# Rounding the fill's operands on GpSimd instead of VectorE, and turning -max and 1/sum a step later

## The chip, the cores and the metric

The kernel runs on one core of one Trainium2 chip. The core has TensorE (PE, with its weight loads PEld), VectorE (DVE), ScalarE (ACT), GpSimd (POOL) and SyncE (SP), which here issues every transfer. Each engine works through its own queue in order and waits for the others by semaphores. The metric is the device time of one execution in microseconds.

## The reference

Two independent layers share one launch, and their outputs are laid side by side. A is attention with 32 query heads of width 32 and a single key and value head, over 2048 rows of width 1024, followed by an output projection. B is a Fourier mixing layer, written as products with cosine and sine matrices.

```
q = (x @ wq).reshape(B, S, H, Dh).transpose(0, 2, 1, 3)      # H = 32, Dh = 32
k = x @ wk;  v = x @ wv
scores = einsum("bhqd,bkd->bhqk", q, k) * Dh ** -0.5
o = einsum("bhqk,bkd->bhqd", softmax(scores), v)
A = o.transpose(0, 2, 1, 3).reshape(B, S, H * Dh) @ wo

a = einsum("bsd,ed->bse", x, dft_hid_re)
b = einsum("bsd,ed->bse", x, dft_hid_im)
B = einsum("ts,bse->bte", dft_seq_re, a) - einsum("ts,bse->bte", dft_seq_im, b)
out = concatenate([A, B], axis=-1)
```

All inputs and outputs are float32.

## The kernel before, in words

Matrix products are made in a rounded float32 form (F32R in the code). To keep the precision, each operand x is split into a high part, x rounded, and a low part, x minus the high part. A product of two operands is then three products on TensorE: high by high, low by high, high by low.

**The fill.** The projections, both stages of the Fourier layer and the output projection are written as a list of groups. A group is one output tile of 128 x 512 and takes 12 or 24 products. The list runs: q, k and v projections; stage 1 of the Fourier layer (the seven products of STAGE1); stage 2 (the seven of PRODUCTS, each in two halves of eight groups); the output projection. The position in this list, counted in products, is `pos["fill"]`.

**The lines that prepare operands.** Two objects of class Line, RL for right operands (tiles rh, rl) and ML for left operands (mh, ml), carry each item through four steps: load (a transfer into r or m), comb (GpSimd adds or subtracts a second or third source, where the item has several), hi (the high part, by `hi_r` or `hi_m`, which call `cast`), and lo (the low part, a subtraction on GpSimd). Each step is issued when the fill has come within a lead of the item's due position: (40, 40, 14, 8) products for RL, (52, 36, 27, 21) for ML. A left operand is due when it is used, and serves 12 products. A right operand serves all eight groups of its half set, and its due position is spread over the set before. Up to the position START (the first groups) `cast` runs on ScalarE and the low part on VectorE; from there `cast` runs on VectorE and the low part on GpSimd. There are 14 buffers for each of rh and rl, 4 for each of mh and ml, 3 and 2 for the first and second source of r and of m.

**The groups' ends.** When a group's last product is placed, its `post` runs. In the second half of a product of stage 2 VectorE adds the PSUM tile to h, and GpSimd adds h into the one or two running sums y that the product touches, where these already exist. Of the two-source left operands, PRODUCTS[0], [1], [3], [4], [5] have them; two running sums are added in PRODUCTS[3] and [6], one in [1], [2], [4] and [5], none in [0]. Stores are issued nine products after their place (BEHIND).

**Attention around it.** The attention runs in 32 units (four blocks of rows by eight groups of heads) of 32 steps. One step of the main loop makes a scores product (tile pss) for a later unit, of which VectorE takes the negated maximum (tile nm) and ScalarE the row sums by an exponential; and a product of the transposed scores (tile pst) for the current unit, of which ScalarE makes the exponential into p. Every eighth step `pv` multiplies 32 pieces of p with v. Fill products are put between by `level`, equally many in every eight steps, none in the step of a pv. There is a bank of PSUM for a group in work and one for what comes between (`bank`).

**The turning.** The transposed scores need -max of each row along the free dimension, and the output needs 1/sum. `lse_1`, `lse_1b` and `lse_2` work these out on VectorE and ScalarE in tile m2 (m in the profile); `lse_3` turns m2 on TensorE with the identity matrix and copies it to mt on VectorE; `lse_4` sends mt with three transfers from SyncE: high and low part of -max into two rows of qst, and 1/sum to the tensor r_d. A unit's transposed scores start at its step 0, in the main loop's count; `lse_3` stands in step 25 of the unit before, one step after a pv, and `lse_4` in step 27. `inverse` fetches 1/sum at step 16 of the unit itself. `aside` completes a group that is just begun or nearly done before anything else uses a bank.

The class Ordered hands every operation to the scheduler in program order, so that the order of each queue is the order of the calls. It records them all, so the profile gives line 66 for nearly everything, and operations are told apart by their tiles.

Of the kernel before, what the change touches and what calls it, by code (L numbers as in the profile page):

```python
# [87 lines left out]
def tile_kernel(ctx: ExitStack, tc, xT, wq, wkv, wo, xbT, wT, cT, out):  # L88
# [3 lines left out]
    dve = Ordered(tc, nc.vector)  # L92
    gp = Ordered(tc, nc.gpsimd)
# [80 lines left out]
    def cast(to, of):  # L174
        if pos["fill"] < START:
            act.activation(to, of, AF.Copy)
        else:
            dve.tensor_copy(to, of)

    def load_r(it):  # L180
        if it.pre or it.t:
# [37 lines left out]
    def hi_r(it):  # L219
        it.hi = rp.tile([P, W], F32R, name="rh")  # L220
        it.lo = rp.tile([P, W], F32R, name="rl")
        if it.pre:
            fetch(it)
        else:
            cast(it.hi, it.t[0])

    def hi_m(it):
        it.hi = mp.tile([P, 4, P], F32R, name="mh")
        it.lo = mp.tile([P, 4, P], F32R, name="ml")
        if it.pre:  # L230
            fetch(it)
            return
        _, n, w = it.t[0].shape
        it.hi, it.lo = it.hi[:, :n, :w], it.lo[:, :n, :w]
        cast(it.hi, it.t[0])
# [355 lines left out]
    def open_unit(u):  # L591
        b, g = units[u]
        assert ("q", b, g) in ready
        q = qsp.tile([P, 4, W], F32R, name="qst")
        gp.memset(q[96:P].bitcast(F32), 0.0)
        for r, src in enumerate((qh_d, ql_d, qh_d)):
            move(sp, q[r * DH:(r + 1) * DH], src[b][g].rearrange("(h d) c -> d h c", d=DH))
        qst[u] = q
        nm[u] = sm.tile([P, 2, NC], F32, name="nm")
        ls[u] = sm.tile([P, 2, NC], F32, name="ls")  # L600

    def scores(s):
        u, r = divmod(s, SU)
        i, j = divmod(r, 2)
        h, t = divmod(i, 4)
        ps = ps_s.tile([P, 2 * W], F32, name="pss")
        for a in range(2):
            k0 = (2 * j + a) * W
            te.matmul(ps[:, a * W:(a + 1) * W], qst[u][:, h, t * P:(t + 1) * P], kst[:, k0:k0 + W], start=True, stop=True)
        dve.tensor_reduce(nm[u][:, j, i:i + 1], ps, axis=AX.X, op=ALU.max, negate=True)  # L610
        pend[s] = ps

    def row_sums(s):
        if s not in pend:
            return
        ps = pend.pop(s)
        u, r = divmod(s, SU)
        i, j = divmod(r, 2)
        act.activation(ps, ps, AF.Exp, bias=nm[u][:, j, i:i + 1], accum_out=ls[u][:, j, i:i + 1])

    def lse_1(u):
        m = sm.tile([P, NC], F32, name="mm")
        d = sm.tile([P, 2, NC], F32, name="md")
        dve.tensor_tensor(m, nm[u][:, 0], nm[u][:, 1], op=ALU.min)
        for j in range(2):
            dve.tensor_sub(d[:, j], m, nm[u][:, j])
        lse[u] = m, d

    def lse_1b(u):
        act.activation(lse[u][1], lse[u][1], AF.Exp)  # L630

    def lse_2(u):
        m, d = lse[u]
        l = sm.tile([P, NC], F32, name="l")
        m2 = sm.tile([P, 3, NC], F32, name="m2")
        dve.tensor_mul(d, d, ls[u])
        dve.tensor_add(l, d[:, 0], d[:, 1])
        dve.tensor_copy(m2[:, 0].bitcast(F32R), m)
        dve.tensor_sub(m2[:, 1], m, m2[:, 0])
        dve.reciprocal(m2[:, 2], l)  # L640
        lse[u] = m2

    def lse_3(u):
        m2 = lse.pop(u)
        aside()
        pm = bank("psb")
        te.transpose(pm[:3 * NC, :P], m2.rearrange("p a b -> p (a b)"), ident)
        mt = sm.tile([3 * NC, P], F32, name="mt")
        dve.tensor_copy(mt, pm[:3 * NC, :P])
        cur["at"] += 1  # L650
        lse[u] = mt

    def lse_4(u):
        mt = lse.pop(u)
        for a in range(2):
            move(sp, qst[u][96 + a:97 + a].rearrange("o h (t c) -> o (h t) c", c=P), mt[a * NC:(a + 1) * NC])
        sp.dma_start(r_d[u], mt[2 * NC:])
# [45 lines left out]
    def score_step(s):  # L703

        if s < total:
            u, r = divmod(s, SU)
            if r == SU - 6 and u + 1 < len(units):
                open_unit(u + 1)
            scores(s)
        row_sums(s - 1)  # L710
        u, e = divmod(s - SU, SU)
        if 0 <= u < len(units):
            if e == 1:
                lse_1(u)
            elif e == 2:
                lse_1b(u)
            elif e == 3:
                lse_2(u)
            elif e == 5:
                lse_3(u)  # L720
            elif e == 7:
                lse_4(u)


# [11 lines left out]
    for s in range(SU + LEAD):  # L736
        score_step(s)
        take(7)
# [14 lines left out]
    for n in range(total):  # L753
        u, r = divmod(n, SU)
        if n == total - 12:
            w1 = wo_set(1)
            add([o_group(NQ - 1, t, e, ws) for e, ws in ((0, w0), (1, w1)) for t in range(4)])
        score_step(n + SU + LEAD)
        if ends:
            ends.pop(0)()  # L760
        expo(n)
        if r == 16:
            inverse(u)
        if r % 8 == 0 and n:
            pv(*divmod(n // 8 - 1, 4))
        level(n)
# [72 lines left out]
```

## Time and profile before

| | |
|---|---|
| median of 3 runs | 2849.58 us (2846.28 to 2852.26) |
| the profiled execution | 2849.53 us, of which the span is 2847.8 us |
| granted TensorE clock, mean | 0.997 |
| TensorE busy | 2794.1 us, 98% |
| ScalarE busy | 2185.7 us, 77% |
| VectorE busy | 1948.0 us, 68% |
| GpSimd busy | 1212.5 us, 43% |
| the 291 roundings of m on VectorE | 167.1 us, 574 ns each |
| the 214 roundings of r on VectorE | 123.1 us, 575 ns each |
| the 32 transpositions of -max and 1/sum on TensorE | 9.1 us, 286 ns each |

How to read it. A group of instructions is named by engine, operation and "out<-in" with buffer numbers left out, so `mh<-m` is the rounding of a left operand. After the bar stand the busy time, the mean of one in ns, and the idle time of the engine just before these instructions with what ended it. In the list of waits a line gives the waiting engine and tile, the releaser, the total in us, the number of times and the longest. A line of the timeline gives start, duration, engine, instruction, and in brackets the idle time before it. PEld is TensorE's loading of weights, which runs beside its products. The ends of matmuls are modelled, so a busy share of 98% doesn't mean that TensorE never stood still; the steps' pace tells that better.

### The profile page before, as it was taken

To read this page: it belongs to the slowest core of one execution; us is meant where nothing else is said; L and a number is where in the kernel's file an instruction comes from. 1 tells how busy PE (TensorE), PEld (TensorE's weight loads), DVE (VectorE), ACT (ScalarE), POOL (GpSimd) and SP (SyncE) were. 2 spreads that over 40 slices of the span, in tenths; PEclk is the share of its full clock that TensorE was granted. 3 is DMA by queue.
4 is the path that set the end of the run, shared out by engine and by line. 5 is a ranking of instruction groups with operands and counts; after the bars stand their busy time and mean duration, and the time that the engine had idled before them with its cause. 6 is when DMAs were issued, how large, how long until landed. Compare 5 with 4: busy or idle time off the path is not lost.

```text
span 2847.8 us, 39945 instructions
## 1 busy us (share of the span) xinstructions
PE 2794.1 (98%) x13904; PEld 1929.8 (68%) x13904; DVE 1948.0 (68%) x2430; ACT 2185.7 (77%) x3151; POOL 1212.5 (43%) x928
## 2 busy tenths in 40 slices
PE   7999999999999999999999999999999999999999
PEld 5776676767666767676767666666666666667656
DVE  6876677777777777776777677677777676766511
ACT  4578788878787888888888888778788788888740
POOL 1211123454324346555664455766666753520000
PEclk9999999999999999999999999999999999999999
DMA  8865425765576455554552454654555533554445
GB/s 295 294 198 172 149 101 167 237 213 197 193 233 212 163 178 160 154 169 123 170 175 93 134 156 133 200 172 138 176 167 155 174 113 100 160 155 138 126 141 170
DMA packets 315722, 480.83 MB, mean 169 GB/s; under 512 B 33408, under 2 KB 98432, under 8 KB 315520
## 3 DMA queue, kind: packets, MB, share of 16 engines
q1 hardware_dynamic: 315520, 478.28, 52.8%
q8 instruction: 109, 1.79, 0.3%
q14 instruction: 93, 0.76, 0.1%
HBM read 364.12 MB, written 112.98 MB: 168 GB/s over the span
## 4 chain that ended last, share of the span: by engine, by line
PE 83%; DVE 7%; ACT 3%; DMA 3%; issue 2%; POOL 1%; SPq 1%; POOLq 0%; ACTq 0%; DVEq 0%
PE psb L66 53%; PE pss L66 15%; PE pst L66 15%; DVE nm L66 2%; ACT pss L66 1%; ACT p L66 1%; DMA ql<-ql 1%; DVE mh L66 1%; DVE rh L66 1%; DVE ov L66 1%; SPq L66 1%; POOL m L66 0%; DMA r<-s 0%; POOL ml L66 0%; DVE md L66 0%
## 5 line engine op out<-in xcount | busy, mean ns | idle before, releaser
L66 DVE TENSOR_REDUCE nm<-pss 128x1 f32<-128x1024 f32 x1024 | 1248.5, 1221 | 379.4 <-PE pss L66 376.6
L66 ACT ACTIVATE p<-pst 128x1024 f32<-128x1024 f32 x1024 | 1051.9, 1027 | 429.4 <-PE pst L66 426.5
L66 ACT ACTIVATE pss<-pss,nm 128x1024 f32<-128x1024 f32 x1024 | 1113.9, 1088 | 149.1 <-DVE nm L66 142.2
L66 PE MATMUL psb<-rh,mh 128*128 128x512 f32 (+1 forms) x1852 | 731.6, 395 | 12.0 <-ACT rh L66 8.2
L66 PE MATMUL psb<-rh,ml 128*128 128x512 f32 (+1 forms) x1852 | 731.9, 395 | 0.7 <-POOL ml L66 0.7
L66 PE MATMUL psb<-rl,mh 128*128 128x512 f32 (+1 forms) x1852 | 729.9, 394 | 0.3 <-DVE rl L66 0.3
L66 PE MATMUL pss<-kst,qst 128*128 128x512 f32 x2048 | 658.6, 403 | 17.2 <-ACT pss L66 16.6
L66 PE MATMUL pst<-qst,kst 128*128 128x512 f32 x2048 | 659.7, 403 | 10.2 <-ACT p L66 9.2
L66 POOL TENSOR_TENSOR rl<-r,rh 128x512 fp32r<-128x512 f32 x214 | 281.9, 1318 | 736.3 <-DVE rh L66 537.8
L66 POOL TENSOR_TENSOR ml<-m,mh 128x512 fp32r<-128x512 f32 x292 | 383.8, 1315 | 484.4 <-DVE mh L66 247.0
L66 PEld LDWEIGHTS pss<-kst,qst 128*128 128x128 f32 x2048 | 373.0, 188 | 208.2 <-issue 93.9
L66 PE MATMUL psb<-p,v 128*32 128x512 f32 x4096 | 466.5, 596 | 0.6 <-DVE h L66 0.5
L66 PEld LDWEIGHTS pst<-qst,kst 128*128 128x128 f32 x2048 | 372.7, 189 | 136.2 <-ACT p L66 54.5
L66 PEld LDWEIGHTS psb<-rh,mh 128*128 128x128 f32 (+1 forms) x1852 | 347.6, 188 | 97.5 <-ACT rh L66 8.7
L66 PEld LDWEIGHTS psb<-rh,ml 128*128 128x128 f32 (+1 forms) x1852 | 347.6, 188 | 84.1 <-POOL ml L66 1.1
L66 PEld LDWEIGHTS psb<-rl,mh 128*128 128x128 f32 (+1 forms) x1852 | 347.3, 188 | 84.5 <-DVE rl L66 1.6
L66 PEld LDWEIGHTS psb<-p,v 128*32 128x32 f32 x4096 | 120.2, 110 | 277.3 <-issue 258.0
L66 POOL TENSOR_TENSOR m<-m,m 128x512 f32<-128x512 f32 x192 | 252.6, 1316 | 13.2 <-DMA m<-in_cT_dram 7.8
L66 DVE TENSOR_TENSOR ov<-ov,psb 128x512 f32<-128x512 f32 x96 | 66.0, 688 | 265.9 <-PE psb L66 265.7
L66 POOL TENSOR_TENSOR r<-r,r 128x512 f32<-128x512 f32 x112 | 149.0, 1331 | 199.1 <-DMA r<-in_wT_dram 101.7
L66 ACT ACTIVATION_READ_ACCUMULATOR pss<-pss,nm 128x1 f32 x1024 | 208.6, 204 | 0.0
L66 DVE CAST mh<-m 128x512 fp32r<-128x512 f32 x291 | 167.1, 574 | 17.5 <-POOL m L66 10.6
(68 smaller groups left out, 848.6 us busy)
## 6 DMA issues: line engine op xcount, KB each, us to landing
m<-in_cT_dram SPq DMA_DIRECT2D x384, 256.0 KB, 3.7
r<-s SPq DMA_DIRECT2D x192, 256.0 KB, 4.3
y<-y SPq DMA_DIRECT2D x96, 256.0 KB, 4.4
r<-in_wT_dram SPq DMA_DIRECT2D x80, 256.0 KB, 3.8
m<-in_xbT_dram SPq DMA_DIRECT2D x80, 256.0 KB, 4.2
y<-u SPq DMA_DIRECT2D x80, 256.0 KB, 2.9
qst<-qh SPq DMA_DIRECT2D x64, 256.0 KB, 5.5
s<-y SPq DMA_DIRECT2D x64, 256.0 KB, 3.5
```

What stands on the lines that cost most here:

```text
L66: return lambda *a, **k: self.tc.keep_in_program_order(f(*a, **k))
```

## The change

Two things are changed. `cast`, which makes the high parts, runs on GpSimd instead of VectorE from the position START on; its place in the program, the leads and the buffers stay. GpSimd thus makes the high part and, some products later, the low part. And the calls of `lse_3` and `lse_4` come one step later, at e == 6 and 8 in place of 5 and 7, that is in steps 26 and 28.

```diff
     def cast(to, of):
         if pos["fill"] < START:
             act.activation(to, of, AF.Copy)
         else:
-            dve.tensor_copy(to, of)
+            gp.tensor_copy(to, of)
...
             elif e == 3:
                 lse_2(u)
-            elif e == 5:
+            elif e == 6:
                 lse_3(u)
-            elif e == 7:
+            elif e == 8:
                 lse_4(u)
```

All other queues keep their contents; the order on TensorE and SyncE shifts slightly around the moved calls.

## The prediction

> **What bounds the kernel now.** First the page: TensorE is busy nearly everywhere, GpSimd only here and there (its row of slices has 4 to 6 tenths in the second half and 0 at the end).
>
> ```profile
> span 2847.8 us, 39945 instructions
> PE 2794.1 (98%) x13904; PEld 1929.8 (68%) x13904; DVE 1948.0 (68%) x2430; ACT 2185.7 (77%) x3151; POOL 1212.5 (43%) x928
> PE   7999999999999999999999999999999999999999
> POOL 1211123454324346555664455766666753520000
> ```
>
> Then the pace. Every unit of attention (32 steps) makes 32 exponentials of the transposed scores, so stretches bounded by those exponentials compare like with like. The windows below give length, ScalarE's busy time with its count, clock, DMA share.
>
> ```profile
> 900.50:1549.40 648.90, 262.95 (x256) 1.00 0.50 157
> 1549.50:2478.70 929.20, 361.51 (x352) 0.99 0.49 150
> 1714.30:1800.50 86.20, 32.77 (x32) 1.00 0.43 134
> 1800.60:1892.20 91.60, 32.88 (x32) 0.96 0.64 203
> 2227.10:2314.20 87.10, 32.82 (x32) 0.98 0.51 158
> ```
>
> Eight units in the middle take 648.9 us, 81.1 each. The eleven after them take 929.2, where 11 x 81.1 = 892 was due: 37 us are lost there, 10.5 in one unit (1800 to 1892). The 81.1 is paced by TensorE and ScalarE together; what the change can win is above all these 37 us.
>
> Third, the waits of 1780 to 1900 us and the timeline inside it:
>
> ```profile
> POOL y L66 <- DVE h L66: 23.1, 7, 7.2
> ACT pss L66 <- DVE nm L66: 16.6, 6, 3.9
> DVE mh L66 <- POOL m L66: 8.4, 4, 2.7
> POOL r L66 <- DMA r<-s: 7.9, 3, 3.4
> PE pss L66 <- ACT pss L66: 7.0, 3, 3.0
> ```
>
> ```profile
> 1833.17 0.67 DVE L66 TENSOR_TENSOR h<-h,psb 128x512 f32<-128x512 f32 x1
> 1833.92 2.54 POOL L66 TENSOR_TENSOR y<-y,h 128x512 f32<-128x512 f32 x2 [2.09 <-DVE h L66]
> 1836.42 1.29 POOL L66 TENSOR_TENSOR m<-m,m 128x512 f32<-128x512 f32 x1
> 1837.67 1.29 POOL L66 TENSOR_TENSOR ml<-m,mh 128x512 fp32r<-128x512 f32 x1
> 1837.75 1.50 DVE L66 CAST mh<-m 128x512 fp32r<-128x512 f32 x1 [2.68 <-POOL m L66]
> 1839.17 1.21 DVE L66 TENSOR_REDUCE nm<-pss 128x1 f32<-128x1024 f32 x1
> 1840.30 0.41 DVE L66 CAST rh<-r 128x512 fp32r<-128x512 f32 x1
> 1840.47 1.09 ACT L66 ACTIVATE pss<-pss,nm 128x1024 f32<-128x1024 f32 x1 [3.00 <-DVE nm L66]
> 1842.65 0.79 PE L66 MATMUL pst<-qst,kst 128*128 128x512 f32 x2 [0.18 <-ACT p L66]
> ```
>
> This is a ring of two queues. GpSimd waits for VectorE's h at a group's end, adds two y, then the next m; VectorE meanwhile has come to the rounding of that m, stands still for 2.68 us, takes 1.50 us instead of 0.41 for it (GpSimd's other work runs beside), and only then reduces the scores that ScalarE waits 3.00 us for. TensorE waits behind ScalarE. VectorE's total of 68% shows none of it.
>
> **The change, part by part.** The by-shape view has the durations, and two rows to bound a GpSimd copy:
>
> ```profile
> L66 DVE CAST mh<-m 128x512 fp32r<-128x512 f32 x291 | 167.1, 574 | 17.5 <-POOL m L66 10.6 <-DMA m<-in_wq_dram 5.9 <-DMA ql<-ql 0.4
> L66 DVE CAST rh<-r 128x512 fp32r<-128x512 f32 x214 | 123.1, 575 | 24.6 <-PE pss L66 14.6 <-DMA r<-in_wo_dram 7.2 <-DMA r<-in_xT_dram 2.9
> L66 POOL TENSOR_TENSOR ml<-m,mh 128x512 fp32r<-128x512 f32 x292 | 383.8, 1315 | 484.4 <-DVE mh L66 247.0 <-issue 71.0 <-PE pss L66 53.8
> L66 POOL MEMSET qst<- 32x2048 f32 x32 | 58.6, 1832 | 1.9
> masks.py:199 POOL TENSOR_SCALAR_AFFINE_SELECT ident<-ident 128x128 f32<-128x128 f32 x1 | 0.3, 292 | 0.1
> masks.py:197 POOL MEMSET ident<- 128x128 f32 x1 | 0.2, 204 | 0.3 <-POOLq L829 0.3
> POOL r L66 <- DMA r<-s: 74.9, 38, 5.9
> PEld psb L66 <- POOL ml L66: 1.1, 1, 1.1
> ```
>
> *505 roundings leave VectorE*: 167 + 123 = 290 us of its 1948. By itself that is worth nothing, since 81.1 us per unit holds whatever VectorE does; the ring above is what ends.
>
> *505 copies come to GpSimd*, each of c us, a form that this trace does not have there. Below, a memset: (1832 - 204) / (2048 - 128) = 0.848 ns per element with 0.095 us fixed, so 512 elements are 0.53 us. Above, the two-input subtraction, 1.32 us. The nearest row reads one tensor, the select on 128 elements: 0.088 us more than the memset of that shape. Put to the fixed part that gives 0.62 us, put to the elements 0.88. I take c = 0.75, so 379 us in all, GpSimd at 1591 us or 56%. Whether it is hidden is a matter of the fullest stretch. A fill of 154 products per unit (4.8 per step, from the code's levelling) is 6.42 groups of 24, so a group lasts 81.1 / 6.42 = 12.64 us. In the second half of PRODUCTS[3] each group has on GpSimd two y, two m, two ml, one r, one rl: 8 x 1.25 us (1836.42 to 1837.67), and 1.83 / 6.42 = 0.29 of the memset, 10.3 together. Three copies of 0.75 make 12.55: just full. The second halves of PRODUCTS[1], [4] and [5] have one y less: 11.3. The r addition also waits for its transfer, 74.9 us over 64 such additions, 1.2 each: 13.75 and 12.5.
>
> *The wait that goes, and what is late next.* m is added 36 products ahead of its use, rounded 27 ahead, and its low part taken 21 ahead. Today VectorE stops when GpSimd is over 9 products (4.7 us) late. Afterwards nobody but TensorE waits, at the use: 21 products, 11.1 us after the low part's place. In the loop shown ml ends 5.8 us after the group's end, with its place 1.6 us after it; so some 6 us of lateness remain free (today TensorE's loads waited for ml only 1.1 us in the whole run). In the PRODUCTS[3] half lateness grows by 13.75 - 12.64 = 1.1 us per group, 9 us over eight, of which 6 are covered: 3 us. Bunched fill (the products stop while a pv runs) I put at another 7. So 10 of the 37 remain: **-27 us**. With c = 0.53 nothing need remain (-37); with c = 1.32 see the first rival.
>
> Behind a waiting copy on GpSimd stand y, m, r and the memset of the next qst. SyncE waits for them in its own order: y stores, and loads into the three m buffers. The memset is wanted six steps, 15 us (2.53 each, 81.1 / 32), later, which covers it; without that the first scores of a unit would wait up to its 1.83 us.
>
> *The beginning.* With the fill alone on TensorE a rounding can lie straight on the path:
>
> ```profile
> 58.44 0.43 DVE L66 CAST mh<-m 128x512 fp32r<-128x512 f32 x1 [3.84 <-DMA m<-in_wq_dram]
> 58.92 0.50 PE L66 MATMUL psb<-rh,mh 128*128 128x512 f32 x1 [1.26 <-DVE mh L66]
> ```
>
> Here 0.75 - 0.43 = 0.3 us is added, three or four times until the loads run ahead: **+1 us** (0 to +4, the latter by 1.32 - 0.43). The end has six roundings among transfers and TensorE work: 0.
>
> *The turning, one step later.* It stands in the step after a pv, and waits for VectorE to empty pv's bank:
>
> ```profile
> 2208.78 0.73 PE L66 MATMUL pss<-kst,qst 128*128 128x512 f32 x2
> 2208.92 0.69 DVE L66 TENSOR_TENSOR ov<-ov,psb 128x512 f32<-128x512 f32 x1 [2.63 <-PE psb L66]
> 2209.66 0.10 PEld L66 LDWEIGHTS psb<-ident,m 128*48 128x48 f32 x1 [0.58 <-DVE ov L66]
> 2210.99 1.15 SPq L66 DMA_DIRECT2D qst<-mt  x2
> L66 PEld LDWEIGHTS psb<-ident,m 128*48 128x48 f32 x32 | 3.3, 102 | 14.5 <-DVE ov L66 13.2 <-issue 0.8
> L66 PE MATMUL psb<-ident,m 128*48 128x128 f32 x32 | 9.1, 286 | 4.1 <-DVE ov L66 1.3
> qst<-mt SPq DMA_DIRECT2D x64, 8.0 KB, 1.8
> ```
>
> The two scores products start at 2208.78, and then the load of the transposition stands idle for 0.58 us until ov is added. Over all 32 the load row books 13.2 us for this wait, the matmul row 4.1 us of idle time in all. One step later the bank is free. I take the matmul row, **-4 us**, since part of the wait only moves to ScalarE; ends -13 and +3 (a wait of 0.1 per unit at the new place). With it go the copy of mt on VectorE (same work), the fill that aside() pulls forward (same work), and three transfers on SyncE. The rows of qst must land by step 32 of a unit; they are now sent at step 28: 4 x 2.53 = 10.1 us, less 1.15 issue and 1.8 landing, 7 us to spare against SyncE being held up. r is fetched twenty steps later. Cost 0.
>
> Sum: 2849.5 (profiled execution; the median is 2849.6) - 27 + 1 - 4 = **2820 us**. Own range of this case 2803 (-37, -10) to 2834 (c near 1.0 leaves 25 instead of 10).
>
> On the price of the copy, the Trainium skill (GPSIMD Engine Reference, Engine selection) says that with one input GpSimd is roughly at line rate; at its 1.2 GHz an estimate is 0.43 us plus a fixed part. By that alone nothing would remain of the 37 and the sum would be 2810. The same page speaks against the change under Key points: for elementwise work VectorE is about twice as fast. Twice the 0.41 us is 0.82, by which some 12 would remain, 2822; no row here shows which holds.
>
> **Rivals.** (1) GpSimd becomes the clock of the fill. Place: second halves of PRODUCTS[1], [3], [4], [5]. At c = 1.32 their groups need 10.3 + 4.0 + 1.2 = 15.5 and 14.2 us against 12.64: 8 x 2.9 + 24 x 1.6 = 61, the lighter halves between add about 5, and 6 us of slack in each of two stretches take off 12: 54 instead of 37. 2849.5 + 17 + 3 - 4 = **2865**. It decides from c of about 1.2, where the excess equals what is won. For it: the select by its elements is already 0.88, and each copy waits for the addition just before it on its own engine. Against: one input only. (2) The 37 us stay, because GpSimd's waits for h and r pace these stretches and not VectorE's standing still: only the 4 us come, **2846**. For it: 23.1 us of waiting for h in 120. Against: the 3.00 us of ScalarE's wait end with VectorE's late reduction. (3) SyncE, held by GpSimd's late work over 7 us, sends -max too late, and the transposed scores wait in the six slow units, some 3 us each: **2838**.
>
> **How the numbers follow.** Forecast 0.56, (1) 0.22, (2) 0.15, (3) 0.07. 0.2% is 5.7 us, about what a measurement of this kernel can tell from no change. Slower: (1) and a little of (2), 0.24; same: most of (2), 0.09; faster 0.67. The range runs from 2803 to rival (1), 2864; both signs lie in it.
>
> **What would show it.** Right: VectorE's rows mh and rh gone, the wait of mh for m with them; units between 1549 and 2478 near 82 us; GpSimd's copy at 0.6 to 0.9 us; no wait of the transposition for ov. Wrong: TensorE waiting for ml, rl or mh in long pieces, a copy above 1.2 us, or pst waiting for qst's transfer.

## The result, and the profile after

The changed kernel took 2831.48 us, median of four runs (2827.57 to 2835.39), where the kernel before took 2850.47 beside it: a ratio of 0.9935, with an interval of 0.9922 to 0.9949. That is 19 us faster. In a second set of runs (e9 below) the same kernel gave 2829.82 us and 0.9932 (0.992 to 0.9943). The forecast was 2820, so the sign was right and some 11 us of the gain did not come.

The profiled execution took 2835.39 us. It is the slowest of the four, and so are the profiled executions of e1 (2833.59 us) and e2 (2848.76) among theirs; windows add up to the span of their own execution and not to the median. The head of its page:

```profile
span 2833.5 us, 40225 instructions
PE 2780.5 (98%) x13904; PEld 1931.6 (68%) x13904; DVE 1733.6 (61%) x1925; ACT 2187.6 (77%) x3151; POOL 1481.7 (52%) x1433
PE   7999999999999999999999999999999999999999
POOL 2321134565534447767685565787888765630010
```

VectorE has lost 505 instructions and GpSimd has gained 505. VectorE's busy time falls by 214 us, and not by the 290 of the roundings. Neighbouring instructions overlap in the records; by the sums of the groups' durations (2052.5 us before, 1787.6 after) it is 265, so what is left on VectorE has become 25 us longer. GpSimd is at 5 to 8 tenths through most of the second half, 52% over all. The group view by shape prices the new copies, and shows the load and the matmul of the turning:

```profile
L66 POOL CAST mh<-m 128x512 fp32r<-128x512 f32 x291 | 182.8, 628 | 195.3 <-PE psb L66 175.2 <-DMA m<-in_xbT_dram 13.2 <-DMA m<-in_wq_dram 5.4
L66 POOL CAST rh<-r 128x512 fp32r<-128x512 f32 x214 | 133.7, 625 | 550.4 <-PE psb L66 191.2 <-PE pst L66 138.2 <-DMA r<-in_wo_dram 70.2
L66 PE MATMUL psb<-ident,m 128*48 128x128 f32 x32 | 8.7, 271 | 0.0
L66 PEld LDWEIGHTS psb<-ident,m 128*48 128x48 f32 x32 | 3.3, 102 | 1.4
```

A copy took 0.63 us. The load of the transposition stood idle for 14.5 us in all before, and now for 1.4. Here are the stretches bounded by the exponentials of the transposed scores (length, ScalarE's busy time in them with its count, clock, DMA share, GB/s): to the end of the third unit, units 9 to 16, units 17 to 27, and one unit of that last stretch.

```profile
0.00:409.70 409.70, 109.81 (x114) 0.99 0.62 203
898.50:1551.70 653.20, 262.87 (x257) 1.00 0.49 156
1551.80:2465.20 913.40, 361.32 (x352) 0.99 0.50 153
1632.50:1721.00 88.50, 32.74 (x32) 0.96 0.49 147
```

The eleven units that took 929.2 us take 913.4, where 892 was due. So the main stretch gained 16 us and still loses 21. Units 9 to 16, which were even at 81.1 us per unit, are 4 us longer than before, and the beginning is 4 us longer. The stretch between the first and the second row gained 6: from the end of the first to the start of the second there are 488.8 us, and 494.9 in the kernel before (900.5 less 405.6, the end of its first three units, whose row stands under e2). The four sum up to nearly all of the 14 us between the two spans.

### The profile page after: what moved, and what is told of

It reads as the page before. It is cut to its first block, busy times and chain, and to the rows that moved or that the text cites. A ratio compares the mean times of both kernels' runs of the same rounds, so it can differ in the third digit from the quotient of the medians.

```text
span 2833.5 us, 40225 instructions
## 1 busy us (share of the span) xinstructions
PE 2780.5 (98%) x13904; PEld 1931.6 (68%) x13904; DVE 1733.6 (61%) x1925; ACT 2187.6 (77%) x3151; POOL 1481.7 (52%) x1433
## 4 chain that ended last, share of the span: by engine, by line
PE 90%; DVE 3%; DMA 3%; ACT 1%; issue 1%; SPq 1%; POOL 0%; ACTq 0%; DVEq 0%; POOLq 0%
PE psb L66 57%; PE pss L66 17%; PE pst L66 16%; DVE nm L66 1%; SPq L66 1%; DMA s<-y 1%; DMA ql<-ql 1%; ACT p L66 1%; DVE md L66 1%; ACT pss L66 0%; DMA p<-in_xT_dram 0%; DVE mm L66 0%; DVE y L66 0%; DMA r<-s 0%; DMA r<-in_xT_dram 0%
## 5 line engine op out<-in xcount | busy, mean ns | idle before, releaser
L66 POOL CAST rh<-r 128x512 fp32r<-128x512 f32 x214 | 133.7, 625 | 550.4 <-PE psb L66 191.2
L66 POOL CAST mh<-m 128x512 fp32r<-128x512 f32 x291 | 182.8, 628 | 195.3 <-PE psb L66 175.2
```

What stands on the lines that cost most here:

```text
L66: return lambda *a, **k: self.tc.keep_in_program_order(f(*a, **k))
```

## The experiments

The kernel "before" beside each run had medians of 2849.2 to 2850.5 us. "After" is the changed kernel. Ratios are to before, with a 95% interval.

### Each part alone: e1 and e2

e1 is the rounding without the later turning, e2 the turning without the rounding on GpSimd.

```diff
e1, against after:
-            elif e == 6:
+            elif e == 5:
                 lse_3(u)
-            elif e == 8:
+            elif e == 7:
                 lse_4(u)

e2, against after:
-            gp.tensor_copy(to, of)
+            dve.tensor_copy(to, of)
```

> Only the rounding is on GpSimd, the turning stands where it stood. Theory A (the ring of VectorE waiting for m and GpSimd waiting for h ends, and that is the gain): some 16 of the 19 us, 2834 us, transposition still waiting 13 us in its load row. Rival B (the turning is the gain): 2847 us.

> Only the turning is a step later, the rounding stays on VectorE. Theory A: 3 us less than before, 2847 us, and the waits of mh for m as before (8 us or more between 1780 and 1900 us). Rival B: 2834 us. Either way the load row of the transposition should lose its 13 us of waiting for ov.

e1: 2825.39 us, 0.9922 (0.9907 to 0.9937). e2: 2844.88 us, 0.9982 (0.9972 to 0.9992). So the rounding alone gives 25 us, where 16 was expected, and the turning alone 5; together they give no more than the rounding alone (the intervals of e1 and of after overlap). Where the turning pays and where it costs is seen in part in the windows, first of the kernel before, then of e2:

```profile
0.00:405.60 405.60, 109.96 (x114) 1.00 0.62 205
2559.70:2640.60 80.90, 32.81 (x32) 1.00 0.47 139
```

```profile
0.00:409.50 409.50, 109.93 (x114) 0.99 0.63 203
2559.60:2640.10 80.50, 32.79 (x32) 1.00 0.47 137
```

A quiet unit late in the run becomes 0.4 us shorter, where the prediction's 4 us over 32 units make 0.1. But the first three units become 4 us longer, and it is the turning that does it, since e1 has the old length there. (Units 9 to 16 are longer too in this execution of e2, 657.7 us from 897.3 to 1555.1 us, where the kernel before took 648.9; why was not followed.) The windows of e1:

```profile
0.00:405.70 405.70, 110.01 (x114) 0.99 0.62 205
1555.20:2462.40 907.20, 361.37 (x352) 1.00 0.50 154
```

One place of these 4 us in e2 is a product of the fill that waits for another piece of work on VectorE, which the later turning now stands beside:

```profile
153.65 0.50 PE L66 MATMUL psb<-rh,mh 128*128 128x512 f32 x1 [1.61 <-DVE ql L66]
```

The other pieces were not followed one by one; 3.3 of the 4 us have come by the first transposed exponential, which starts at 163.7 us before and at 166.9 in e2. The first row of e1's windows also settles the rounding's own cost at the beginning: 0.1 us, where the prediction took 1. Its second row is the main stretch with the rounding alone: 907.2, that is 22 less than before.

### Which of VectorE's roundings matter: e3 and e4

In e3 only the 291 roundings of left operands go to GpSimd, and the 214 of right operands stay on VectorE (the turning as in after). In e4 all roundings stay on VectorE and the kernel is the one before, but the rounding of a left operand is called 22 products ahead of its use in place of 27.

```diff
e3, against after:
-    def cast(to, of):
+    def cast(to, of, eng=None):
...
-            gp.tensor_copy(to, of)
+            (eng or dve).tensor_copy(to, of)
...
-        cast(it.hi, it.t[0])
+        cast(it.hi, it.t[0], gp)

e4, against before:
-    ML = Line(NM0, NM, (52, 36, 27, 21), load_m, comb, hi_m, lo)
+    ML = Line(NM0, NM, (52, 36, 22, 21), load_m, comb, hi_m, lo)
```

> The left operands (291) are rounded on GpSimd, the right ones (214) stay on VectorE, the turning is a step later. Theory A: VectorE stood still for m alone, so the whole gain comes, 2832 us or a little less since GpSimd has 214 copies fewer. Rival C (what counts is VectorE's time, 290 us off its queue): 291/505 of the rounding's 16 us, 2838 us.

> The kernel before, with the left operands' rounding called 22 products ahead of its use in place of 27, still on VectorE; nothing else moves. Theory A: VectorE comes to it some 2.6 us later, about as long as it stood still at most (2.68 us), so most of the ring's cost goes: 2838 us. Rival C (VectorE's time and the slowed copies): nothing of that changes, 2850 us.

e3: 2827.99 us, 0.9927 (0.9914 to 0.9941), the whole gain of after. e4: 2834.22 us, 0.9951 (0.9938 to 0.9964): 16 us by one number, with VectorE's work unchanged. The waits of VectorE for GpSimd's sums m, in the kernel before, and the same line in e2, where the rounding is still on VectorE:

```profile
DVE mh L66 <- POOL m L66: 10.6, 8, 2.7
```

```profile
DVE mh L66 <- POOL m L66: 11.6, 11, 2.4
```

In e4 the view of VectorE's waits has no such line. What e4 does with the stretch of units 17 to 27, and e3 after it:

```profile
1557.50:2463.30 905.80, 361.69 (x352) 1.00 0.50 154
```

```profile
1551.60:2457.30 905.70, 361.62 (x352) 1.00 0.50 154
```

Both stand at 906, and e1 at 907. So the ring that the prediction described is shown. It is broken when VectorE stops standing still in front of m, whether the rounding goes to another engine or only stands five products later in VectorE's own queue. The 127.4 us of right roundings that e3 leaves on VectorE are worth nothing that could be measured, and neither were the 290 us as a sum. All three still stand 14 or 15 us above the 892 that was due, and e4 is one of them, in which no copy has moved to GpSimd.

### The price of the copy: e5

Each copy is made twice, so it costs 1.25 us and everything else stays.

```diff
             gp.tensor_copy(to, of)
+            gp.tensor_copy(to, of)
```

> The changed kernel with every rounding on GpSimd done twice into the same tile, so that a copy costs about 1.25 us of GpSimd's queue in place of 0.63. If GpSimd becomes the clock of the fill (the prediction's first rival, decided at 1.2 us): 2850 us or more, with TensorE waiting for ml, rl or mh by name. If the margin of some 6 us covers it: under 2838 us.

2858.55 us, 1.0033 (1.0023 to 1.0043): 27 us above after and 9 above before. The group of left copies and, from the list of waits, what TensorE and its weight loads now wait for:

```profile
L66 POOL CAST mh<-m 128x512 fp32r<-128x512 f32 x582 | 364.8, 627 | 110.4 <-PE psb L66 81.8 <-DMA m<-in_xbT_dram 5.9 <-DMA m<-in_wq_dram 3.5
```

```profile
PEld psb L66 <- POOL ml L66: 32.2, 25, 3.1
PE psb L66 <- POOL ml L66: 19.0, 17, 2.6
PE pst L66 <- DMA qst<-mt: 6.0, 3, 2.5
```

In after, the middle line reads 3.5 us in 4 times. So the mechanism of the first rival exists, by name, at twice the copy's real price. An estimate by a straight line between these two runs, -19 us at 0.63 and +9 at 1.25, puts the point where nothing is won at about 1.05; the prediction had it at 1.2. The last line is the third rival's mechanism, 6 us at this price. In after it shows once:

```profile
1887.95 0.70 PE L66 MATMUL pst<-qst,kst 128*128 128x512 f32 x2 [1.51 <-DMA qst<-mt]
```

### What still loses 15 to 21 us: e6, e7 and e8

TensorE waits little for low parts in after, so what remains of the 37 us is something else. The slow unit at 1632.5 to 1721 us of after (88.5 us) shows it in the timeline:

```profile
1687.25 5.78 DVE L66 TENSOR_TENSOR mm<-nm 128x16 f32<-128x16 f32 x1
1688.16 0.61 POOL L66 CAST mh<-m 128x512 fp32r<-128x512 f32 x1
...
1690.52 1.26 POOL L66 TENSOR_TENSOR ml<-m,mh 128x512 fp32r<-128x512 f32 x1
1691.74 1.26 POOL L66 TENSOR_TENSOR rl<-r,rh 128x512 fp32r<-128x512 f32 x1
...
1693.07 0.26 DVE L66 TENSOR_TENSOR md<-mm,nm 128x16 f32<-128x16 f32 x2
...
1694.56 1.22 PE L66 MATMUL pst<-qst,kst 128*128 128x512 f32 x2 [4.31 <-ACT p L66]
...
1696.76 0.61 POOL L66 CAST mh<-m 128x512 fp32r<-128x512 f32 x1 [3.77 <-PE psb L66]
```

A minimum of two pieces of 128 x 16, some tenths of a microsecond of work, stands on VectorE for 5.78 us. GpSimd runs without a gap meanwhile. The operation ends at 1693.03, when GpSimd's subtraction for rl has ended and GpSimd itself has to wait for TensorE. ScalarE waits for the differences behind this minimum, and TensorE 4.31 us for ScalarE. It is a ring again, at another place. A hold of this length is rare: in e9, the same kernel once more, none of these small operations stood longer than 1.33 us, about one GpSimd instruction with two inputs (1.29 us). But the two subtractions md<-mm,nm, one behind the other, took 2.44 to 2.47 us together five times there.

The operations of this kind grew in the group view. Before:

```profile
L66 DVE TENSOR_TENSOR md<-mm,nm 128x16 f32<-128x16 f32 x64 | 22.1, 385 | 1.1
L66 DVE TENSOR_TENSOR mm<-nm 128x16 f32<-128x16 f32 x32 | 11.9, 372 | 0.0
L66 DVE CAST m<-mm 128x16 fp32r<-128x16 f32 x32 | 7.6, 238 | 0.0
```

After:

```profile
L66 DVE TENSOR_TENSOR md<-mm,nm 128x16 f32<-128x16 f32 x64 | 26.6, 456 | 1.1
L66 DVE TENSOR_TENSOR mm<-nm 128x16 f32<-128x16 f32 x32 | 18.7, 586 | 0.0
L66 DVE CAST m<-mm 128x16 fp32r<-128x16 f32 x32 | 12.3, 384 | 0.0
```

Of the 18.7 us of the minimum, 5.78 are the one long hold. In e9 the three means are 547, 453 and 456 ns.

The Trainium skill (SBUF — State Buffer, Who interferes with whom) states that a VectorE operation with two inputs in SBUF contends with a GpSimd operation that reads SBUF, and that a reduction never contends on this chip. The test follows that: the minimum and the sum are made as reductions over a view of one tensor, and the two subtractions as one. e6 does this on top of after, e7 on top of before, e8 on top of e1.

```diff
-        dve.tensor_tensor(m, nm[u][:, 0], nm[u][:, 1], op=ALU.min)
-        for j in range(2):
-            dve.tensor_sub(d[:, j], m, nm[u][:, j])
+        dve.tensor_reduce(m, nm[u].rearrange("p j i -> p i j"), axis=AX.X, op=ALU.min)
+        dve.tensor_sub(d, m.unsqueeze(1).to_broadcast([P, 2, NC]), nm[u])
...
-        dve.tensor_add(l, d[:, 0], d[:, 1])
+        dve.tensor_reduce(l, d.rearrange("p j i -> p i j"), axis=AX.X, op=ALU.add)
```

> The changed kernel with three of VectorE's small two-operand steps in lse_1 and lse_2 replaced: the minimum and the sum over the two halves by a reduction with one input, and the two subtractions by one; same values. Theory D (what remains of the loss are small operations with two inputs from SBUF that VectorE cannot do while GpSimd runs without a gap, one of 5.78 us at 1687 us): the longest such operation drops under 3 us, some 6 to 9 us less, 2824 us. Rival E (they are long by chance, and what is lost comes back elsewhere, for h or ml): 2831 us.

> The kernel before with VectorE's fewer small two-operand steps and nothing else. Theory D (their price is that they are held off while GpSimd runs, and that the change made this worse): 4 to 6 us less, 2845 us. Rival F (they cost the same before the change, as instructions between two reductions of scores): the 17 us that they gave on the changed kernel come here too, 2833 us.

> Rounding on GpSimd and the fewer steps, with the turning where it stood before. If the turning is worth on top of the rounding what it is alone (5 us): 2819 us, against 2814 with it. If its 4 us of loss in the first units and its gain per unit cancel there: 2813 to 2815 us. If it costs: 2809 us.

e6: 2814.41 us, 0.9877 (0.9863 to 0.9892). e7: 2843.47 us, 0.9981 (0.9973 to 0.9989). e8: 2813.8 us, 0.988 (0.9865 to 0.9894). The same edit takes 17 us off after, 12 off e1, and 6 off the kernel before. ScalarE's wait for the differences behind the minimum follows these gains. Here it is in the lists of waits of before, e4, e1 and after, in this order; e6, e7 and e8 have no such line:

```profile
ACT md L66 <- DVE md L66: 5.1, 7, 1.9
ACT md L66 <- DVE md L66: 9.5, 10, 2.0
ACT md L66 <- DVE md L66: 12.3, 14, 1.7
ACT md L66 <- DVE md L66: 13.9, 11, 4.7
```

Where 5.1, 12.3 and 13.9 us of this wait go, the time falls by 6, 12 and 17. Some 6 us could thus be had already before the change. That the moved copies alone made the wait grow is not shown: in e4 it is 9.5 us, with every rounding on VectorE. The reductions on top of e4 were not run. In e6 the two reductions, and the stretch of units 17 to 27:

```profile
L66 DVE TENSOR_REDUCE l<-md 128x16 f32<-128x32 f32 x32 | 6.0, 188 | 1.1
L66 DVE TENSOR_REDUCE mm<-nm 128x16 f32<-128x32 f32 x32 | 5.7, 179 | 0.0
```

```profile
1546.50:2445.50 899.00, 361.55 (x352) 1.00 0.50 156
```

The reduction for the minimum takes 0.18 us with GpSimd beside it, none of the 32 over 0.181, where the minimum that it replaces took 0.37 on the mean before, 0.59 in after and 0.45 in e9; in this trace the page's rule holds. The edit also makes one subtraction out of two, and what each part gave was not separated. The stretch is at 899, 7 above what was due. e6 and e8 beat both kernels; between them no difference could be measured, so the later turning is worth nothing here either.

### Changed again: e9

e9 is after itself once more, beside e7 and e8.

> The changed kernel itself once more, on the chip of the other runs of this call, for a narrower interval beside the run of the rounding alone (0.9922 of before). If the turning adds its 5 us: 0.991. If it adds nothing: 0.992 to 0.994.

2829.82 us, 0.9932 (0.992 to 0.9943). Its stretch of units 17 to 27 took 907 us, not 913: part of the 21 us that the first profile showed is the spread from one execution to the next.

### Taking GpSimd's own wait away: e10, e11 and e12

GpSimd waited 155.8 us for the second source of r in e6. e10 is e6 with r loaded 52 products ahead of its due position in place of 40.

```diff
-    RL = Line(NR0, NR, (40, 40, 14, 8), load_r, comb, hi_r, lo)
+    RL = Line(NR0, NR, (52, 40, 14, 8), load_r, comb, hi_r, lo)
```

> The changed kernel with the fewer steps, and the right operands loaded 52 products ahead in place of 40, so that GpSimd's addition no longer waits for its transfer (156 us in the run with the fewer steps). If GpSimd's lateness still costs TensorE something there: 2808 us or less. If these waits only fill time in which GpSimd had nothing to do: 2814 us.

2839.23 us, 0.9964 (0.9951 to 0.9976): 25 us slower than e6, where both expectations had 2814 or less. Units 17 to 27 took 923 us in place of 899. The wait did go, as the lists of e6 and then e10 show:

```profile
POOL r L66 <- DMA r<-s: 155.8, 55, 12.0
```

```profile
POOL r L66 <- DMA r<-s: 49.5, 9, 11.8
```

But it seems to have been a gap in which VectorE came to its turn. From the timeline of e10 (between the second and the third line GpSimd ran ten more instructions with no pause):

```profile
1882.05 13.65 DVE L66 TENSOR_TENSOR ov<-ov,rb 128x512 f32<-128x512 f32 x1
1882.36 1.31 POOL L66 TENSOR_TENSOR m<-m,m 128x512 f32<-128x512 f32 x1
...
1893.88 1.27 POOL L66 TENSOR_TENSOR r<-r,r 128x512 f32<-128x512 f32 x1
...
1898.19 1.22 PE L66 MATMUL pss<-kst,qst 128*128 128x512 f32 x2 [11.53 <-ACT pss L66]
...
2191.30 8.70 DVE L66 TENSOR_TENSOR md<-md,ls 128x32 f32<-128x32 f32 x1
```

A multiplication that took 0.81 us on the mean in e6 stands for 13.65, and TensorE waits 11.53 behind it. e11 puts a short GpSimd instruction that reads nothing behind each copy of e10, and e12 does so behind each copy of e8:

```diff
+    gap = keep.tile([P, 128], F32, name="gap")
...
             gp.tensor_copy(to, of)
+            gp.memset(gap, 0.0)
```

> The kernel with the earlier loads (2839 us, in which two operations of VectorE with two inputs from SBUF lasted 13.65 and 8.70 us beside a GpSimd that ran without a gap), with a memset of 128 x 128 on GpSimd, which reads nothing, behind each rounding: 505 of about 0.2 us. Theory D (VectorE's second input waits for a gap in GpSimd's reading): no such operation over 3 us, and 2815 to 2822 us although GpSimd has 100 us more to do. Rival G (the earlier loads cost for another reason, such as SyncE's order): 2839 us or more.

> Rounding on GpSimd, fewer two-operand steps, the turning where it stood before, and the same memset behind each rounding. Theory D: the remaining held operations of 1.2 us get shorter, 2808 to 2814 us. Rival G, or a GpSimd too full to take 100 us more: 2816 us or more.

e11: 2818.97 us, 0.9901 (0.9879 to 0.9924). e12: 2817.44 us, 0.9884 (0.9867 to 0.99). In e11, 104 us more work on GpSimd made the kernel 20 us faster than e10:

```profile
L66 POOL MEMSET gap<- 128x128 f32 x505 | 104.1, 206 | 0.0
```

That a gap in GpSimd's reading lets VectorE go is thereby supported, but not all that was expected came. The profiled execution of e11 (2831.19 us, where the other three took 2818 to 2820) still holds a multiplication for 5.68 us and another operation for 13.18, and this one is a cast with a single input:

```profile
1880.25 5.68 DVE L66 TENSOR_TENSOR ov<-ov,rb 128x512 f32<-128x512 f32 x1
...
2100.99 13.18 DVE L66 CAST m<-mm 128x16 fp32r<-128x16 f32 x1
```

The multiplication ended 0.4 us after the next memset. The cast stood past three memsets and ended only when GpSimd came to wait. On e8, where GpSimd still waits 155 us for r's second source, the gaps bring nothing (0.9884 against 0.988), though 2808 to 2814 us was expected: the cast m<-mm took 0.66 us on the mean in place of 0.52, and TensorE's loads waited 11.2 us for ml in place of 6.6. What exactly lets a held operation in, and whether the cast is held by another rule than the operations with two inputs, stays open.

## Why the prediction was right or wrong, point by point

- **The ring and what ends it** (the -27): right in mechanism. VectorE's wait for m is gone, e1 gains 22 us in the stretch where it stood, e3 shows that the left copies alone do it, and e4 that the place in the queue does it without GpSimd. Rival 2, that the 37 us stay, has fallen.
- **What is late next** ("So 10 of the 37 remain"): this step failed in its mechanism, and its number was too low. In the profiled executions of e1, e3, e4, e9 and after, 14 to 21 us remained. The prediction reckoned with 3 us of TensorE waiting for GpSimd's low parts and 7 for bunched fill. The first came as forecast, 3.5 us in the products themselves; the second no run tested. Left out were VectorE's own small operations, held while GpSimd works, and ScalarE's wait behind them, 13.9 us in after against 5.1 before. e6 shows it, by taking 17 us off after without touching GpSimd's program. That the moved copies closed GpSimd's gaps can be only a part of it, since e4, which moves none, has 14 us left too and 9.5 us of this wait. The sign stood in the prediction's own quotation, the rounding that took 1.50 us in place of 0.41 beside GpSimd; the prediction counted that as a cost which leaves VectorE, and not as a price that VectorE's remaining operations pay.
- **Units 9 to 16**: costed at nothing, since they were even. They became 4 us longer in after and 6 in e9 (654.9 us), but 6 in e4 (654.8) and 9 in e2 as well, with every rounding on VectorE, so the moved copies cannot be the whole cause. With the two reductions they took 649.3 us in e6 and e8, nearly as before the change (648.9). What made them longer stays open.
- **The copy, c = 0.75**: it was 0.625 us by the right operands and 0.628 by the left, the lower of the two values that the select on 128 elements gave (0.62, its excess put to the fixed part). The Trainium skill (GPSIMD Engine Reference, Engine selection) has one-input work roughly at line rate; the estimate of 0.43 us agrees with 0.625 if the fixed part is 0.2 us, which no row shows apart, and twice VectorE's 0.41 does not agree. GpSimd came to 1481.7 us in place of 1591. By the prediction's own working 0.63 us makes GpSimd 0.7 us late per group, 6 over eight, which its margin covers; the 7 us of bunched fill would be left and some 2817 us come out, as an estimate. That did not come, so the price did not set the remainder.
- **Rival 1, GpSimd as the clock**: did not happen at 0.63 us. At 1.25 it happens as described (e5). Its deciding point was put too high, 1.2 against about 1.05 by the estimate under e5.
- **The beginning, +1**: 0.1 us by e1 for the rounding. The turning's share, 4 us in the first three units, was not costed at all.
- **The turning, -4**: alone it gives 5 (e2), and the transposition no longer waits for ov. That the size is met is partly luck, since 4 us at the beginning go against it. On top of the rounding it gives nothing that could be measured (e1 against after, e8 against e6).
- **SyncE's 7 us to spare, cost 0**: held but for one wait of 1.51 us. Rival 3's wait comes to 6.0 us at e5's price, in three places.
- **VectorE's 290 us worth nothing by themselves**: right, by e3 and e4.

In the sum: 2849.5 - 27 + 1 - 4 was forecast. By the medians the rounding gives -25 (e1), close to its -26, and the turning on top gives nothing (after and e9 stand 4 to 6 us above e1, and the intervals overlap) in place of -4. So by the medians the missing 11 us lie mostly in the turning. That the rounding's term was nearly met is partly luck, since other waits remained than those reckoned: e1's profiled execution gained 16 us, 22 in units 17 to 27 with 5 lost in units 9 to 16. The 17 us that e6 takes off after are more than what is missing to 2820. The lower end of the range, 2803, has a -10 beside the -37 that the stated terms do not give.

## What to carry to other kernels

When work is moved from VectorE to GpSimd, count what it does to the gaps in GpSimd's queue. In these runs a VectorE operation with two inputs in SBUF, however small, often stood for a whole GpSimd instruction (1.3 us) and now and then until GpSimd paused; on a chain that TensorE waits behind, write a minimum or a sum of two pieces as a reduction over one tensor. And look for a rounding or a copy that stands too early in an in-order queue before moving it to another engine: here one lead, 27 to 22, gave 16 of the 25 us.

## What the runs showed of the hardware that was not expected

- A VectorE operation on 128 x 16 elements stood for 5.78 us, one on 128 x 32 for 8.70, one on 128 x 512 for 13.65, each beside a GpSimd queue that ran without a pause. The Trainium skill (SBUF — State Buffer, Summary: rules for kernel authors) has the one who comes second blocked until the first finishes. The holds of up to 1.33 us in e9 agree with that; these three lasted over several GpSimd instructions, the longest over a dozen in a row.
- Removing a wait of GpSimd (156 us down to 50) made the kernel 25 us slower, and adding 104 us of work that reads nothing to the same queue made it 20 us faster.
- A cast with one input, 128 x 16, stood for 13.18 us in e11, past three of the memsets that had been put in as gaps.
